# Loading and scoring the first pair of heads one head at a time, in a windowed attention and gated MLP kernel

## The chip, the cores and the metric

The kernel runs on one core of a Trainium2 chip. The metric is the device time of one execution in microseconds (us). The core has a matrix engine (TensorE; PE for its matmuls and PEld for its weight loads in the profile), a vector engine (VectorE, DVE), a scalar engine (ScalarE, ACT), GpSimd (POOL) and a queue engine (SyncE, SP) from which nearly all transfers between HBM and the on-chip memory are issued. The engines run their own instruction streams in order and wait for each other by semaphores.

## The reference

For 8 sequences (batch) of 576 tokens, 8 heads of 64 channels each, attention is computed with a causal window, and its result goes through an MLP with a gate:

```python
scores = scale * np.matmul(q, k.transpose(0, 1, 3, 2))        # [8, 8, 576, 576]
rel = pos[:, None] - pos[None, :]
mask_plain = (rel >= 0) & (rel < 32)                          # heads 0 to 3
mask_dil = (rel >= 0) & (rel < 128) & (rel % 4 == 0)          # heads 4 to 7
attn = softmax(np.where(masks, scores, -1e9))
x = np.matmul(attn, v) reshaped to [4608 tokens, 512]
h = x @ w_in                                                  # 512 -> 2048
return (h * sigmoid(1.702 * h)) @ w_out                       # 2048 -> 512
```

All inputs and the output are float32. Every query sees at most 32 keys.

## The kernel before, in words

Two heads are one "pair" (128 partitions: 64 channels of the one head, 64 of the other), so there are 32 pairs, four for each batch, numbered k = 0 to 31. `qk[k]` holds queries and keys of a pair, transposed, as 128 rows of 1152 floats. Pair 0 is the first thing that the kernel works on.

For a pair the steps are: load queries and keys (`load_qk`, line 425), load values (`load_v`, line 439), write the mask into a two-bank PSUM tile `sp` by a matmul with the identity (line 478) and add 42 small score matmuls for each head (line 490), both in `scores` (line 471); then on DVE the row maximum (line 510) and its subtraction out of PSUM (line 512, in the helper of line 353), on ACT the exponential (line 514), on DVE the sum and the reciprocal (lines 526 and 518), on POOL the two multiplications by it (line 529), on DVE two transposes (line 695), and the product with the values on PE (`first_product`, line 560, matmuls of line 576). The result is split into a high and a low part in `xs` by ACT (line 650) and DVE (line 652). The PSUM tile `sp` exists once: scores of pair k+1 start when the subtraction of pair k has read it. `first_product` writes a PSUM tile `first_x`, of which two pairs share the columns.

Weights come in as 64-bit words of w_in and w_out. `decode` (line 363) loads one 128 x 512 block (`fetch`, line 392) and turns it into a high and a low part: three operations that are ACT's for the first blocks (lines 402, 403, 396), shifts and adds on DVE or POOL (lines 406, 408), then the copy and the remainder (lines 409, 410). The MLP's up-projection (matmuls of line 863, three for each product, because high and low parts are multiplied apart) starts as soon as the first quarter of `xs` and the first w_in block are there. From then on PE is meant to be always busy.

What order the work has is written by a planner in the kernel's own code (`Plan`, lines 48 to 213). Every operation is given to it with a cost per engine that may do it, an urgency (the smaller, the earlier), the names that it reads and writes, a "slack" before which it isn't started, and, on PE, a count of instructions. `placed` (line 111) walks through time: it takes the engine whose next operation could start first, and among the operations that could start by then on this engine the one with the smallest urgency. Transfers go to SP's queue in the order of urgency as far as their inputs allow. For transfers it counts bytes over a common bus (line 203). The result is the program order of each engine; on the chip each engine keeps that order whatever the real durations are. The four first pairs have, for queries and keys, the urgencies -9.0, -5.7, -4.7 and -2.3, and for values -6.7, -6.7, -3.8 and -1.6 (the last three with a slack of 4, 11 and 14). The first weight blocks w_in 0, w_in 1, w_out 0 and w_in 2 have -7.8, -5.7, -4.6 and -2.5. `scores` of pairs 0 to 3 has an urgency of about -100000, so PE does it as soon as it can.

In the first 60 us the planner also fills PE's gaps with matmuls on constants (`warm`, line 1253): small ones of line 1262, each of which is two matmuls and two weight loads in the program, and large ones of line 1258. It keeps account of blocks of PE instructions: a first block of 193 and further ones of 256 (`fetched`, line 134), where the next block can be entered only some time after the last one was (4.2 or 6.1 in its own model); small fillers are put in up to such an edge (line 188).

The transfers' semaphores come from the framework, as do all waits: it follows which part of which tile an instruction reads and writes.

The functions that the change touches, and what calls them:

Of the kernel before, what the change touches and what calls it, by code (L numbers as in the profile page):

```python
# [15 lines left out]
B, H, S, D = 8, 8, 576, 64  # L16
DM, DF = 512, 2048
P = 128
NC = DM // P
NF = DF // P  # L20
GT = 512
# [12 lines left out]
QT = 5  # L34
# [182 lines left out]
def tile_windowed_attention_then_gated_mlp(  # L217
# [19 lines left out]
    add = plan.add  # L237
# [7 lines left out]
    def bank(shape, tag, name):  # L245
        return ps.tile(shape, F32, tag=tag, name=name)
# [116 lines left out]
    def decode(n, urgency):  # L363

        out_, f = order[n]
        if out_:
            src, hi, lo, key = w_out[f], wo(f)[:, 0], wo(f)[:, 1], f"wo{f}"
        else:
            src, hi, lo, key = w_in[f], wi(f)[:, 0], wi(f)[:, 1], f"wi{f}"

        r = n if n < 3 else (n - 2) % 5
        R, E = {3: "bt", 4: "qk0"}.get(n, f"cell{r}"), f"words{n % 3}"
        word = words[:, n % 3]  # L380
        taken = {5: ("first qk1",), 6: ("first qk1", "first v1")}.get(n, ())
        value = word.bitcast(F32)
        at = {}

        def fetch(e):
            if n == 3:
                raw = bt_all[:, 0:2 * DM].bitcast(U64)
            else:
                raw = temp([P, DM], U64, "qk", f"cell_{n}") if n == 4 else cells[r]
            at["halves"] = raw.bitcast(U16).rearrange("p (n t) -> p n t", t=4)  # L390
            at["low"], at["top"] = (raw.bitcast(U32).rearrange("p (n t) -> p n t", t=2)[:, :, j] for j in range(2))
            load(raw, src)

        def take_sign(e):
            if e == ACT:
                A.activation(at["halves"][:, :, 1].bitcast(F16), f32(at["top"]), AF.Copy, scale=2.0 ** -112)
            else:
                V.tensor_scalar(out=at["halves"][:, :, 1], in0=at["halves"][:, :, 3], scalar1=0x8000, scalar2=None,
                                op0=ALU.bitwise_and)

        add({DMA: 524}, {0: -7.8, 1: -5.7, 2: -4.6, 3: -2.5}.get(n, urgency), fetch, (), (R, R + "l", *taken))
        add({ACT: 0.66}, urgency, lambda e: A.activation(value, f32(at["top"]), AF.Copy, scale=2.0 ** -112), (R,), (E,))
        add({ACT: 0.66}, urgency, lambda e: A.activation(
            at["low"], at["low"], AF.Copy, scale=2.0 ** -29), (R,), (R + "l",))
        add({DVE: -0.75, ACT: 1.37}, urgency, take_sign, (R,), (R + "l",))
        add({DVE: -0.43}, urgency, lambda e: V.tensor_scalar(
            out=word, in0=word, scalar1=3, scalar2=None, op0=ALU.logical_shift_left), (), (E,))
        add({DVE: -0.70, POOL: 1.33}, urgency, lambda e: pair(e, word, word, at["low"], ALU.add), (R + "l",), (E,))
        add({ACT: 0.62, DVE: -0.42}, urgency, lambda e: copy(e, hi, value), (E,), (key,))
        add({DVE: -0.70, POOL: 1.36}, urgency, lambda e: pair(e, lo, value, f32(hi), ALU.subtract), (E,), (key,))  # L410
# [8 lines left out]
    def lots(k):  # L419

        if 0 < k < NC:
            return f"first qk{k}", f"first v{k}"
        return "qk0", "v0"

    def load_qk(k):
        u, place = pairs[k], lots(k)[0]

        def work(e):
            if 0 < k < NC:
                flat = (None, late, main_x, left_x)[k]  # L430
            else:
                flat = temp([P, 2 * S], F32, "qk", f"qk_{k}")

            u["qk"] = flat[:, 0:2 * S]
            load(u["qk"], qk[k])

        add({DMA: 590}, (-9.0, -5.7, -4.7, -2.3)[k] if k < NC else 1.6 * k - 2.0, work, waits(k), (place, place + "l"))

    def load_v(k):
        u, place = pairs[k], lots(k)[1]  # L440

        def work(e):
# [8 lines left out]
            u["v"] = flat.rearrange("p (a s d) -> p a s d", a=2, s=NB)  # L451
            load(flat, vp[k - NC])

        add({DMA: 390 if k < NC else 328}, (-6.7, -6.7, -3.8, -1.6)[k] if k < NC else 1.6 * k - 0.3, work, waits(k),
            (place, place + "l"), (0.0, 4.0, 11.0, 14.0)[k] if k < NC else 0.0)

    def waits(k):

        return ["xh3.0"] if NC <= k < FIRST * NC else []
# [8 lines left out]

        return k < FIRST * NC

    def scores(k):
        u = pairs[k]
        u["sp"] = bank([P, 2, GT], "sp", f"sp_{k}")
        u["all"] = u["sp"][:, :, 0:QT * W].rearrange("p a (t w) -> p a t w", t=QT)
        u["box"] = [u["all"][:, a] for a in range(2)]
        if masked(k):
            for a in range(2):
                T.matmul(u["box"][a], ident, plain if not dilated(k) else classes if k < NC else mask, start=True,
                         stop=False, skip_group_check=True)
        for t in range(QT):  # L480
            for a, g in [(a, g) for a in range(2) for g in range(4 if k < NC or t < QT - 1 else 2)]:
                rows = slice(D * a, D * a + D)
                dst = u["box"][a][32 * g:32 * g + 32, t]
                at = ROW * g + 32 * t if k < NC else HALF * (g // 2) + W * t + 32 * (g % 2)
# [198 lines left out]
    def first_attention(k):  # L683


        load_qk(k)
        load_v(k)
        add({PE: 1.5 if k else 2.3}, k - 1.0e5, lambda e: scores(k), (lots(k)[0],), ("sp", f"scores{k}"), count=180)
        softmax(k, k)

    def first_transposed(k):
# [621 lines left out]
```

## Time and profile before

| | us |
|---|---|
| median of 3 runs | 823.12 |
| lowest, highest | 821.65, 823.53 |
| the profiled execution's own time | 822.45 |
| its span in the profile | 820.7 |
| PE busy | 809.3 |
| DVE, ACT, POOL busy | 669.0, 518.0, 328.4 |
| PE's granted clock, mean | 0.997 |

The span runs from the first to the last instruction of the profile; the execution's own time is 1.75 us longer. "Busy" on PE includes the fillers, so the gaps of the start are not all seen in it. In rows of the timeline the first number is the start of a group in us, the second its length; a bracket says how long its engine idled before it and what ended that. In the chain of waits, "issue" is time in which an engine waited for nothing that the profile shows.

### The profile page before, as it was taken

The numbers are of one execution on the slowest core, as the hardware profiler recorded it, in microseconds if no ns is written. First come the engines' busy times: TensorE is split into PE (matmuls) and PEld (weight loads), VectorE is DVE, ScalarE is ACT, GpSimd is POOL, SyncE is SP. The second block draws the span as 40 slices with busy tenths as digits, with TensorE's granted clock in tenths as the row PEclk, the third lists the DMA queues.
The fourth block names the chain that finished last, engine by engine and source line by source line (L and its number), as shares of the span: only waits on it lengthen the run. The fifth ranks groups of instructions, "written<-read, shape, count | busy, mean of one in ns | idle before, by whom it ended". The sixth has DMA issues, their size and how long they took to land.

```text
span 820.7 us, 18890 instructions
## 1 busy us (share of the span) xinstructions
PE 809.3 (99%) x7279; PEld 653.4 (80%) x7279; DVE 669.0 (82%) x1081; ACT 518.0 (63%) x988; POOL 328.4 (40%) x294
## 2 busy tenths in 40 slices
PE   7999999999999999999999999999999999999997
PEld 4677878888887888778888888888888888888886
DVE  6898988888888876899889899996679885867575
ACT  7898986767577766786866654545456534544340
POOL 3442325455556553244345445531215332112251
PEclk9999999999999999999999999999999999999999
DMA  9577658899758657797788777775565658674545
GB/s 354 186 249 212 175 161 296 287 318 303 241 176 271 223 180 243 252 307 234 235 236 264 253 254 249 234 256 183 179 207 189 198 189 275 201 226 157 180 153 181
DMA packets 109610, 188.13 MB, mean 229 GB/s; under 512 B 26448, under 2 KB 55376, under 8 KB 109520
## 3 DMA queue, kind: packets, MB, share of 16 engines
q1 hardware_dynamic: 109376, 186.78, 70.2%
q8 instruction: 58, 0.95, 0.5%
q14 instruction: 32, 0.26, 0.1%
q10 hardware_dynamic: 144, 0.13, 0.0%
HBM read 140.64 MB, written 45.09 MB: 226 GB/s over the span
## 4 chain that ended last, share of the span: by engine, by line
PE 97%; DMA 1%; DVE 1%; issue 0%; ACT 0%; SPq 0%; DVEq 0%
PE hp_m L863 16%; PE up_p L1006 10%; PE up_r L1006 9%; PE up_q L1006 9%; PE acc_m L800 5%; PE second_p_Q L1121 5%; PE second_q_Q L1121 5%; PE acc_m L804 5%; PE acc_m L801 5%; PE second_r_Q L1121 5%; PE sp L490 4%; PE second_q_Z L1121 3%; PE second_r_Z L1121 3%; PE second_R L1121 3%; PE second_p_Z L1121 3%; PE av L608 2%
## 5 line engine op out<-in xcount | busy, mean ns | idle before, releaser
L353 POOL TENSOR_TENSOR arena<-arena 128x256 f32<-128x256 f32 (+3 forms) x94 | 100.7, 1083 | 97.8 <-DVE wi_last_units L353 21.6
L863 PE MATMUL hp_m<-xs,wi_kept 128*128 128x512 f32 x504 | 127.7, 396 | 1.2 <-DVE arena L872 0.9
L863 PEld LDWEIGHTS hp_m<-xs,wi_kept 128*128 128x128 f32 x504 | 92.9, 188 | 22.8 <-DVE arena L872 1.9
L353 POOL TENSOR_TENSOR wo_kept<-arena,wo_kept 128x512 fp32r<-128x512 f32 x41 | 56.9, 1395 | 131.5 <-ACT wo_kept L346 84.9
L346 ACT ACTIVATE wo_kept<-arena 128x512 fp32r<-128x512 f32 x111 | 69.2, 630 | 40.7 <-PE second_r_Q L1121 10.9
L1006 PE MATMUL up_r<-wi_kept,xs 128*128 128x512 f32 x336 | 85.3, 389 | 0.0
L1006 PE MATMUL up_p<-wi_kept,xs 128*128 128x512 f32 x336 | 84.2, 394 | 0.2 <-DVE arena L353 0.2
L1006 PE MATMUL up_q<-wi_kept,xs 128*128 128x512 f32 x336 | 83.4, 389 | 0.0
L1006 PEld LDWEIGHTS up_p<-wi_kept,xs 128*128 128x128 f32 x336 | 62.1, 188 | 14.7 <-DVE arena L353 0.9
L1006 PEld LDWEIGHTS up_q<-wi_kept,xs 128*128 128x128 f32 x336 | 63.0, 188 | 13.3 <-DVE arena L1028 0.3
L1006 PEld LDWEIGHTS up_r<-wi_kept,xs 128*128 128x128 f32 x336 | 63.1, 188 | 13.1
L353 DVE TENSOR_TENSOR wo_kept<-arena,wo_kept 128x512 fp32r<-128x512 f32 x80 | 61.1, 775 | 5.1 <-ACT wo_kept L346 4.7
L346 ACT ACTIVATE bt<-ct 32x256 f32<-32x256 f32 (+1 forms) x130 | 56.6, 435 | 11.7 <-DVE ct L534 6.0
L353 POOL TENSOR_TENSOR pr<-pr,sm 128x320 f32<-128x320 f32 x52 | 43.7, 856 | 48.5 <-DVE sm L518 43.5
L800 PE MATMUL acc_m<-gh,wo_kept 128*128 128x512 f32 x156 | 61.5, 394 | 0.0
L353 POOL TENSOR_TENSOR wo_kept<-wi_last_units,wo_kept 128x512 fp32r<-128x512 f32 x22 | 29.9, 1361 | 78.3 <-ACT wo_kept L346 72.3
L353 DVE TENSOR_TENSOR arena<-arena 128x512 f32<-128x512 f32 (+1 forms) x75 | 59.1, 797 | 2.7 <-ACT arena L346 1.8
L801 PE MATMUL acc_m<-gh,wo_kept 128*128 128x512 f32 x156 | 60.8, 390 | 0.0
L1027 ACT ACTIVATE arena<-arena 128x512 f32<-128x512 f32 x60 | 37.4, 628 | 33.4 <-DVE arena L353 27.2
L1028 DVE SCALAR_TENSOR_TENSOR arena<-arena 128x512 f32<-128x512 f32 x60 | 49.8, 837 | 1.7 <-ACT arena L1027 1.3
L346 ACT ACTIVATE gh<-arena 128x512 fp32r<-128x512 f32 x57 | 36.0, 631 | 17.5 <-DVE arena L872 5.8
L353 DVE TENSOR_TENSOR gl<-arena,gh 128x512 fp32r<-128x512 f32 x53 | 41.3, 779 | 6.5 <-ACT gh L346 3.2
(267 smaller groups left out, 1824.7 us busy)
## 6 DMA issues: line engine op xcount, KB each, us to landing
xs<-sums SPq DMA_DIRECT2D x168, 256.0 KB, 3.3
out_weights<-sums_o SPq DMA_DIRECT2D x63, 512.0 KB, 3.5
qk<-qk_dram SPq DMA_DIRECT2D x29, 576.0 KB, 4.4
xs<-sums_o SPq DMA_DIRECT2D x21, 512.0 KB, 3.8
v<-vp_dram SPq DMA_DIRECT2D x28, 320.0 KB, 4.1
sums_o<-arena SPq DMA_DIRECT2D x32, 256.0 KB, 3.2
sums<-arena SPq DMA_DIRECT2D x32, 256.0 KB, 2.9
arena<-wi_dram SPq DMA_DIRECT2D x15, 512.0 KB, 4.7
```

The costliest lines, as they stand in the source:

```text
L346: A.activation(dst, src, AF.Copy, scale=scale)
L353: (V if e == DVE else G).tensor_tensor(out=dst, in0=a, in1=b, op=op)
L490: T.matmul(dst[:, w:w + n], u["qk"][rows, at:at + 32], u["qk"][rows, S + first:S + first + n], start=not masked(k), stop=True, tile_positi ...
L608: T.matmul(u["x"][i][rows, at:at + last - first], u["v"][keys, a, m], bt[keys, m, a, first:last], start=(bank_, a) not in begun, stop=True ...
L800: T.matmul(self.acc[j], w[:, 0, cols], high, start=f == 0, stop=False)
L801: T.matmul(self.acc[j], w[:, 1, cols], high, start=False, stop=False)
L804: T.matmul(self.acc[j], w[:, 0, P * j:P * j + P], low, start=False, stop=f == NF - 1)
L863: T.matmul(hps[f], wi(f)[:, st, cols], mv[:, c], start=c == 0 and k == 0, stop=c == NC - 1 and k == 2)
L1006: T.matmul(self.banks[place], xs[:, slot, at:at + P], wi_kept[:, 2 * a + c, mv], start=fresh and c == 0 and k == 0, stop=c == 1 and k == 2 ...
L1027: add({ACT: 0.60}, -10.0, lambda e: A.activation(unit(tmp), src(), AF.Tanh, scale=0.851), need, own(tmp))
L1028: add({DVE: -0.70 if need[0][0] == "A" else 0.70}, -10.0, lambda e: V.scalar_tensor_tensor(out=unit(dst), in0=unit(tmp), scalar=1.0, in1=s ...
L1121: T.matmul(self.second[key], w[:, st, cols], mv, start=fresh and y == 0 and k == 0, stop=y == 1 and k == 2, skip_group_check=True)
```

## The change

Pair 0's `qk[0]` is loaded by two transfers of 64 rows (one head each) in place of one of 128 rows; they write two names, `qk0` and `head1`, have the same urgency (-9.0) and half the cost in the planner. `scores(0)` is given to the planner as two operations, one for each head, each with its own mask matmul and its 42 score matmuls, at a cost of 0.75 each where the whole had 2.3, and a count of 90 instructions each where the whole had 180. Head 1's operation waits for `head1`. Weight block 4, which is loaded into the same place as `qk[0]`, also takes `head1`. The urgency of pair 0's values goes from -6.7 to -4.5: in the order of urgencies they were third (behind qk 0 and w_in 0), and now qk 1, w_in 1, qk 2 and w_out 0 come ahead of them as well.

```diff
-        taken = {5: ("first qk1",), 6: ("first qk1", "first v1")}.get(n, ())
+        taken = {4: ("head1",), 5: ("first qk1",), 6: ("first qk1", "first v1")}.get(n, ())
...
-        def work(e):
+        def work(e, rows=slice(0, P)):
...
-            u["qk"] = flat[:, 0:2 * S]
-            load(u["qk"], qk[k])
+            if "qk" not in u:
+                u["qk"] = flat[:, 0:2 * S]
+            load(u["qk"][rows], qk[k][rows])
+        if k == 0:
+            for a in range(2):
+                add({DMA: 295}, -9.0, lambda e, a=a: work(e, slice(D * a, D * a + D)), (), (("qk0", "head1")[a],))
+            return
...
-        add({DMA: 390 if k < NC else 328}, (-6.7, -6.7, -3.8, -1.6)[k] if k < NC else 1.6 * k - 0.3, work, waits(k),
+        add({DMA: 390 if k < NC else 328}, (-4.5, -6.7, -3.8, -1.6)[k] if k < NC else 1.6 * k - 0.3, work, waits(k),
...
-    def scores(k):
+    def scores(k, heads=range(2)):
...
-            for a in range(2):
+            for a in heads:
                 T.matmul(u["box"][a], ident, plain if not dilated(k) else classes if k < NC else mask, start=True,
...
-            for a, g in [(a, g) for a in range(2) for g in range(4 if k < NC or t < QT - 1 else 2)]:
+            for a, g in [(a, g) for a in heads for g in range(4 if k < NC or t < QT - 1 else 2)]:
...
-        add({PE: 1.5 if k else 2.3}, k - 1.0e5, lambda e: scores(k), (lots(k)[0],), ("sp", f"scores{k}"), count=180)
+        if k == 0:
+            for a in range(2):
+                add({PE: 0.75}, k - 1.0e5, lambda e, a=a: scores(k, (a,)), (("qk0", "head1")[a],), ("sp", f"scores{k}"), count=90)
+        else:
+            add({PE: 1.5}, k - 1.0e5, lambda e: scores(k), (lots(k)[0],), ("sp", f"scores{k}"), count=180)
```

More of the change, by code (lines that the diff above doesn't have):

```diff
@@ L426, in load_qk @@
         u, place = pairs[k], lots(k)[0]
-        def work(e):
+        def work(e, rows=slice(0, P)):
             if 0 < k < NC:
                 flat = (None, late, main_x, left_x)[k]
-            else:
+            elif "qk" not in u:
                 flat = temp([P, 2 * S], F32, "qk", f"qk_{k}")
-            u["qk"] = flat[:, 0:2 * S]
-            load(u["qk"], qk[k])
+            if "qk" not in u:
[5 more added lines that the diff above has]
+            return
         add({DMA: 590}, (-9.0, -5.7, -4.7, -2.3)[k] if k < NC else 1.6 * k - 2.0, work, waits(k), (place, place + "l"))
@@ L469, in masked @@
         return k < FIRST * NC
-    def scores(k):
+    def scores(k, heads=range(2)):
         u = pairs[k]
-        u["sp"] = bank([P, 2, GT], "sp", f"sp_{k}")
+        if 0 in heads:
+            u["sp"] = bank([P, 2, GT], "sp", f"sp_{k}")
         u["all"] = u["sp"][:, :, 0:QT * W].rearrange("p a (t w) -> p a t w", t=QT)
```

## The prediction

> **What bounds the kernel now.** I read the page first, then the busy times by stretches.
>
> ```profile
> span 820.7 us, 18890 instructions
> 60.00:100.00 40.00, 40.00 (x391) 32.12 (x390) 35.65 (x64) 35.21 (x58) 12.94 (x11) 1.00 0.69 204
> ```
>
> From 60 us on PE (second number) is busy all the time. The change leaves that work alone, so it can move the end only by moving the start: by the time at which PE's real work, not its fillers, gets going. Next I read the chain of waits over the first 26 us.
>
> ```profile
> 1.25 4.70 DMA arena<-wi_dram
> 5.96 0.67 ACT arena L402
> 6.66 0.43 DVE arena L406
> 7.09 0.74 DVE mx L510
> 7.85 0.84 DVE pr L353
> 8.74 0.71 PE sp L478 x2
> 9.45 1.38 PE sp L490 x74
> 10.83 2.67 PE idle L1258 x6
> 13.50 0.53 PE sp L478 x2
> 15.10 2.27 PE idle L1258 x10
> 18.42 1.83 issue
> 20.62 1.42 PE first_x L576 x69
> 22.03 2.56 PE idle L1258 x6
> 24.60 1.09 PE first_x L576 x67
> ```
>
> Two things stand here. Pair 0's maximum (L510) starts at 7.09, not because its scores are late but because a weight operation (L406), fed by w_in 0, is ahead of it on DVE. And PE stops for 1.83 us in the middle of pair 3's scores, waiting for nothing that is seen. PE's timeline says what that is.
>
> ```profile
> 1.02 1.56 PE L1262 MATMUL idle<-ones 32*32 32x16 f32 x98 [1.02 <-DVE ones L309]
> 4.27 0.69 PE L478 MATMUL sp<-plain,ident 128*128 128x320 bf16 x2 [1.69 <-DVE plain L332]
> 4.89 1.45 PE L490 MATMUL sp<-qk 64*32 64x64 f32 x84
> 6.27 0.72 PE L1262 MATMUL idle<-ones 32*32 32x16 f32 x38
> 9.38 1.45 PE L490 MATMUL sp<-arena 64*32 64x64 f32 x84
> 13.97 1.13 PE L490 MATMUL sp<-arena 64*32 64x64 f32 x84
> 17.56 0.86 PE L490 MATMUL sp<-arena 64*32 64x64 f32 x65
> 20.25 0.37 PE L490 MATMUL sp<-arena 64*32 64x64 f32 x19 [1.83 <-issue]
> ```
>
> Up to the stop PE has run 98+2+84+38+2+2+84+6+2+84+10+2+65 = 479 matmuls (the 2s and the 2, 6 and 10 in between are masks and large fillers), and as many weight loads: 958 instructions. The plan's own account of instruction blocks has edges at 193, 449, 705 and 961. So the stop is a block that isn't there yet. Instruction 705 ran about 0.46 us into pair 2's scores, at 14.4; 961 ran at 20.25. A block behind the next edge thus took 5.8 us under full DMA. An estimate of the other end: after 20.25 come 19, 92 and 6 matmuls, 1192 instructions, and edge 1217 falls at about 24.7 without a stop, so there it took no more than 4.45, with a DMA share of 0.81 (the row of 20.80 below).
>
> **Head by head.** PE isn't held by the load of pair 0 for long. Its mask waits until 4.27 for DVE's `plain`, which the change doesn't touch; both masks and scores after that need 0.69 + 1.45, and they end at 6.34 now.
>
> ```profile
> 0.81 0.39 SPq L435 DMA_DIRECT2D qk<-qk_dram  x1
> DMA to landing us min/median/max: 4.1/4.1/4.1
> 45.74 0.43 PE acc_m L800
> 46.17 0.23 PE acc_m L801
> ```
>
> Queries and keys land at 0.81 + 4.1 = 4.9, when the masks are just done. Halved, they gain at most these 0.1 us. The new order mask, scores, mask, scores adds one change from small tiles back to a full one: the first full matmul behind scores takes 0.43, its like 0.23, so 0.20. Scores end at 4.27 + 0.69 + 1.45 + 0.20 = 6.6. For no gain, one more transfer is issued (0.39 of SP); it is hidden, as the loads queue on the DMA engines until 22 us.
>
> The real effect is on the order. In the planner's costs the scores of pair 0 now end about 1.45 earlier (0.75 behind head 1's half, where 2.3 stood), so the maximum and the subtraction go ahead of L406 on DVE. The subtraction ends at 6.6 + 0.05 + 0.82 + 0.02 + 0.84 = 8.35 in place of 8.69. L406 comes 1.7 later, and what hangs on it is w_in 0, first used at 25.6: free. Pair 1 follows: 8.40 + 0.71 + 1.38 = 10.5 in place of 10.83, if its keys are there by 9.1.
>
> **Values later.** The next rows give landings: first values, pair 1's keys.
>
> ```profile
> v<-first_v_dram SPq DMA_DIRECT2D x1, 384.0 KB, 6.2
> arena<-qk_dram SPq DMA_DIRECT2D x3, 576.0 KB, 7.1
> 1.71 0.44 SPq L448 DMA_DIRECT2D v<-first_v_dram  x1
> 2.19 0.43 SPq L435 DMA_DIRECT2D arena<-qk_dram  x1
> ```
>
> Values landed at 7.9, keys 1 at 9.3 (just ahead of the scores at 9.38), w_in 0 at 5.95. Without the values in front, keys 1 land 0.9 (384 of 576 KB by their 1.38) to 1.95 earlier, 7.35 to 8.4. By the urgencies the values are now behind keys 1, w_in 1, keys 2 and w_out 0, four transfers; the same bytes lie ahead of them as of w_out 0 now, so they land near 13.6. Their reader is `first_product` 0, now at 20.55: 7 us of cover; uncovered, it would cost what it lands behind that.
>
> **What takes the gain back.** Two steps, both from the order. On DVE pair 0's sum (L526) runs in the wait for pair 1's scores now:
>
> ```profile
> 7.22 1.34 ACT L396 ACTIVATE arena<-arena 128x512 f16<-128x512 f32 x1
> 9.48 0.83 DVE L526 TENSOR_REDUCE sm<-pr 128x10 f32<-128x650 f32 x1 [0.20 <-ACT pr L514]
> 10.87 0.82 DVE L510 TENSOR_REDUCE mx<-sp 128x10 f32<-128x640 f32 x1 [0.56 <-PE sp L490]
> 11.73 0.82 DVE L353 TENSOR_TENSOR pr<-sp,mx 128x640 f32<-128x640 f32 x1
> ```
>
> The exponential still waits for L396, ACT's weight step, until 8.56. In the planner's costs pair 1's maximum is now ready 0.05 ahead of that sum and so stands before it. With 0.82 and 0.83 of the rows, subtraction 1 then ends at 10.5 + 0.04 + 0.82 + 0.83 + 0.82 = 13.0, where 12.55 is now: 0.45 lost. PE didn't use 12.55, as fillers held it to 13.50; still, the lead is gone.
>
> Second, the blocks. With head 0 planned 0.82 earlier (295 of the bus's 360 a us), only 44 of the 49 double small fillers fit: 176 instructions, short of edge 193. It is now crossed by head 0's scores at about 4.7, not in the fillers at 2.5. Then 172 for the scores, 8 for four large fillers and 4 for masks: edge 449 lies 89 instructions of 168 into pair 1's scores, at 9.1 + 0.53 x 1.38 = 9.8. Plus 5.8: edge 705, inside pair 2's scores, at 15.6 (work alone would be there at 14.4). Plus 5.8: edge 961 at 21.4. With fewer fillers before it, it now lies 57 of 184 instructions into `first_product` 0 (now 38 ahead of it), so that product ends at 21.4 + 0.69 x 1.42 = 22.4, against 22.03: +0.4. Behind it the planner's gap takes 5 large fillers, not 6, of 0.43 each:
>
> ```profile
> 20.80:24.20 3.40, 3.40 (x95) 1.86 (x80) 3.28 (x7) 2.33 (x7) 1.21 (x1) 0.52 0.81 288
> 7.20:10.60 3.40, 2.75 (x87) 1.00 1.01 403
> ```
>
> These are stretches of 3.4 us: PE's busy time behind the length, then at the end the granted clock, the DMA share and GB/s (the second row has PE alone). The clock is halved in the 3.4 us behind the stop; it will be again. Minus 0.43: the sum is -0.03.
>
> Unknown is when the block behind edge 449 comes, as its predecessor is crossed at 4.7. With 4.45 it is there at 9.15 and costs nothing; with 5.8, at 10.5, everything behind is 0.7 later. The DMA of this stretch is as full as where 5.8 was measured, but the queue is filling up still at 4.7; I take about a third, +0.2. From `first_product` 1 on, the drains by ACT and DVE set the pace as now. The profiled execution took 822.45 (1.75 over its span); 822.65 after, and the median of before lies 0.67 higher: 823.3. Own range: -0.6 to +0.9, 822.5 to 824.0.
>
> **Rivals.**
>
> *Faster: no stop.* If blocks take 4.45 here too, pair 2's scores end at 14.5, subtraction 2 at 16.2, pair 3's scores at 17.9, and edge 961 (18.85) stops PE for only 0.5. `first_product` 0 ends near 19.9, 2.2 earlier; with PE always busy its clock stays full, and fillers of 0.23 no longer hold the next product. From 1.5 (values 2 land no earlier than now, near 23) to 2.9 gained: 821.0. For it: gaps between 4.27 and 9 close, and the values make room. Against: the 5.8, measured in just such traffic. The Trainium skill (Runtime: NRT & Kernel Launch, Instruction fetch mechanics) calls the crossing of a 256-instruction block mostly hidden; by that this rival would hold, yet the 1.83 above contradicts it.
>
> *Slower: a stop inside pair 1's scores.* In 7.20:10.60 PE idled 0.65 and the large fillers went on at 0.43 until 13.5. If the block behind 449 arrives at 10.5 or later, that idle time comes back and the clock stays halved; ten fillers, which the longer planned gap takes now in place of six, then last 4.3. Pair 2 starts at 15.5, its scores end at 17.6, edge 961 comes at 23.2, `first_product` 0 ends at 24.2: +2.2, less 0.43: 825.0. It decides from about 0.6 us of idling on.
>
> *Slower loads of half the rows.* No transfer of 64 rows is in this trace. If each half takes as long as the whole, head 1 lands 1.2 later (w_in 0, 512 KB, landed 1.05 behind the whole), at 6.1; scores end at 6.85, keys 1 land at 8.55 to 9.6, all edges move by up to 0.45: 823.8. For none of it is there a row; below nothing is excluded, the bytes being the same. The Trainium skill (SBUF — State Buffer, Door 1: The DMA port swizzle) has partitions 0 to 63 reach only half the ports, at half the rate, and two such transfers hardly overlapping; by it this rival is the case.
>
> *It doesn't do what it says.* If head 0's scores wait for both halves, they end at 4.9 + 0.72 + 0.20 + 0.35 + 0.72 = 6.9: +0.3, 823.6. Against: a half of a tile is followed by itself now, as DVE transposes after the first of two multiplications.
>
> ```profile
> 11.89 1.58 POOL L353 TENSOR_TENSOR pr<-pr,sm 128x320 f32<-128x320 f32 x2 [0.56 <-DVE sm L518]
> 12.82 0.50 DVE L695 STREAM_TRANSPOSE ct<-pr 128x320 f32<-128x320 f32 x1
> ```
>
> **Numbers.** Forecast 0.38, no stop 0.25, stop in pair 1's scores 0.20, slow halves 0.11, no effect of halving 0.06. 0.2% is 1.65 us, about what a measurement of this kernel can tell. Faster by more: most of the first rival and a tail, 0.23; slower by more: most of the second and tails, 0.20; within: 0.57. For 8 in 10 the range reaches to both: 820.9 (past the first rival's 821.0) to 825.2.
>
> **What would show it.** In the changed profile: L510 ahead of L406 on DVE, at 6.6; pair 1's scores ending at 10.5; L526 behind the second L510; 88 small fillers; "issue" gaps inside pair 2's scores near 15 and inside `first_product` 0 until 21.4. No gap at either would make it wrong on the fast side; a gap in pair 1's scores or fillers of 0.43 after 10.6, on the slow side; a head 1 landing after 5.5, on the loads.

## The result and the profile after

The changed kernel takes 830.24 us (829.22 to 832.88), the kernel before in the same comparison 823.04: a ratio of 1.0095 with a 95% interval of 1.0069 to 1.0122; by the medians that is 7.2 us slower. The prediction said 823.3 and no change. The profiled execution, the fastest of the four, took 829.22 us, with a span of 827.5, 6.8 over the span of before.

The page of the changed kernel: its span and the busy times.

```profile
span 827.5 us, 18826 instructions
...
PE 808.3 (98%) x7238; PEld 653.9 (79%) x7238; DVE 666.1 (80%) x1077; ACT 514.2 (62%) x985; POOL 337.5 (41%) x301
```

PE's busy time is not longer (808.3 against 809.3): the 6.8 us are idle time of PE. And POOL has 337.5 us of work where it had 328.4, though nothing in the change touches POOL. Where PE idles is read by stretches. The columns are the stretch, its length, PE's busy time and matmuls, the granted clock, the DMA share and GB/s. The changed kernel:

```profile
26.00:40.00 14.00, 11.47 (x286) 1.00 0.37 98
40.00:60.00 20.00, 19.02 (x218) 1.00 0.81 277
...
120.00:140.00 20.00, 18.39 (x215) 1.00 0.46 150
...
400.00:500.00 100.00, 98.61 (x828) 1.00 0.77 247
```

And the same view of the kernel before, for the stretches that changed most:

```profile
26.00:40.00 14.00, 13.78 (x208) 1.00 0.46 145
...
120.00:140.00 20.00, 20.00 (x231) 1.00 0.74 250
...
400.00:500.00 100.00, 100.00 (x829) 1.00 0.81 258
```

Somewhat more than half of the added idle time lies before 60 us, most of that behind 26; the rest lies far behind the change: PE, which was busy all of the time at 120 to 140 and 400 to 500 us, now idles there for 1.6 and 1.4. The waits of the changed kernel's PE (us in total, times, longest) say for what:

```profile
PE hp_m L874 <- DVE arena L883: 3.5, 3, 1.6
PE first_x L583 <- DVE xs L353: 2.5, 2, 1.3
...
PE first_x L583 <- issue: 1.7, 1, 1.7
PE second_p_Q L1132 <- DVE arena L1153: 1.4, 2, 1.2
PE sp L497 <- issue: 1.2, 1, 1.2
```

The kernel before has no wait of PE for DVE at `first_x` or at `second_p_Q` (the down-projection of the first full block), and at the up-projection `hp_m` only this one:

```profile
PE hp_m L863 <- DVE arena L872: 0.9, 1, 0.9
```

Only the two waits for "issue" belong to the steps that the prediction worked out. The others, 3.5 + 2.5 + 1.4, are waits for results of DVE.

The start as PE ran it in the changed kernel (timeline: start, length, instructions, idle time before in brackets):

```profile
4.70 1.32 PE L497 MATMUL sp<-qk 64*32 64x64 f32 x42
...
6.33 1.32 PE L497 MATMUL sp<-qk 64*32 64x64 f32 x42
...
10.09 1.33 PE L497 MATMUL sp<-arena 64*32 64x64 f32 x84
11.36 2.33 PE L1269 MATMUL idle<-ident 128*128 128x512 bf16 x10
...
14.49 0.99 PE L497 MATMUL sp<-arena 64*32 64x64 f32 x75
16.64 0.33 PE L497 MATMUL sp<-arena 64*32 64x64 f32 x9 [1.16 <-issue]
...
22.83 1.00 PE L583 MATMUL first_x<-ct,v 32*64 32x64 f32 x70 [1.72 <-issue]
...
29.90 1.08 PE L583 MATMUL first_x<-ct,arena 32*64 32x64 f32 x80 [1.22 <-DVE xs L353]
...
34.76 1.08 PE L583 MATMUL first_x<-ct,arena 32*64 32x64 f32 x80 [1.31 <-DVE xs L353]
...
42.47 1.25 PE L874 MATMUL hp_m<-xs,wi_kept 128*128 128x512 f32 x3 [0.94 <-DVE arena L883]
```

The two stops for "issue" stand where the prediction put them. PE has run 351 and 479 matmuls up to them, with the weight loads 702 and 958 instructions; 958 is also where the kernel before stops. The first product ends at 23.83 (22.04 before: +1.8). But then two stops of 1.22 and 1.31 follow that it did not have, both for `xs`, the result of draining `first_x` (ACT and DVE copy it out of PSUM), and one of 0.94 in the up-projection. The reason of the first stands on DVE, in the changed kernel's timeline:

```profile
26.32 1.23 DVE L406 TENSOR_SCALAR arena<-arena 128x512 uint32<-128x512 uint32 x2
...
28.59 0.59 DVE L353 TENSOR_TENSOR xs<-first_x,xs 128x432 fp32r<-128x432 f32 x1
```

Steps on weights (two L406 and, left out here, a remainder of 1.20) stand ahead of the drain that PE waits for. ACT's part of this drain is done at 27.69, DVE's starts at 28.59: 0.9 of the 1.22. The same, with some 0.7, is seen once more at 34.76. To follow the delay through the execution I use the first start of PE's matmuls for three tiles (tile view: count, ns of one, first and last start). Changed kernel, then before:

```profile
L811 PE MATMUL acc_m<-gh,wo_kept x156: 387/389/499, 43.6 to 333.7; 128*128 128x512 f32 x156
L1017 PE MATMUL up_p<-wi_kept,xs x336: 387/389/504, 342.7 to 482.7; 128*128 128x512 f32 x168
L1017 PE MATMUL up_q<-wi_kept,xs x336: 387/389/398, 487.1 to 634.4; 128*128 128x512 f32 x168
```

```profile
L800 PE MATMUL acc_m<-gh,wo_kept x156: 387/389/504, 39.6 to 330.6; 128*128 128x512 f32 x156
L1006 PE MATMUL up_p<-wi_kept,xs x336: 387/389/501, 337.9 to 477.2; 128*128 128x512 f32 x168
L1006 PE MATMUL up_q<-wi_kept,xs x336: 388/389/498, 480.2 to 627.5; 128*128 128x512 f32 x168
```

The delay is 43.6 - 39.6 = 4.0 when the down-projection of the first part starts, 4.8 at the first full block `up_p`, 6.9 at the next one, and 6.8 at the end of the span. So in these two executions 4.0 us are lost in the start and about 3 behind it, where the source of the kernel is unchanged.

What did change there is the order. By the lists that the planner writes, 206 of its 4184 operations are given to another engine than before, and 187 of these start behind 60 us of the planner's own time. The inputs that the change gave it (costs and counts of pair 0's loads and scores, one urgency) make it plan everything anew. How they reach so far stands in its code: it plans four times, and in the last three rounds, behind 130 us of its time, it goes no longer by the urgencies that are given to it but by latest starts that it works out from the start times of the round before (`latest`). By its own costs it expected the changed kernel to end 1.45 us earlier.

### The profile page after: what moved, and what is told of

Its sections match the earlier page's. It is cut to its first block, busy times and chain, and to the rows that moved or that the text cites. A ratio compares the mean times of both kernels' runs of the same rounds, so it can differ in the third digit from the quotient of the medians.

```text
span 827.5 us, 18826 instructions
## 1 busy us (share of the span) xinstructions
PE 808.3 (98%) x7238; PEld 653.9 (79%) x7238; DVE 666.1 (80%) x1077; ACT 514.2 (62%) x985; POOL 337.5 (41%) x301
## 4 chain that ended last, share of the span: by engine, by line
PE 89%; DVE 6%; ACT 2%; issue 2%; DVEq 0%; ACTq 0%
PE hp_m L874 14%; PE up_r L1017 9%; PE up_q L1017 9%; PE up_p L1017 8%; PE second_q_Q L1132 5%; PE second_r_Q L1132 5%; PE acc_m L811 5%; PE acc_m L815 5%; PE acc_m L812 5%; PE second_p_Q L1132 5%; PE sp L497 3%; PE second_r_Z L1132 3%; PE second_R L1132 3%; PE second_q_Z L1132 3%; PE second_p_Z L1132 2%; PE av L615 2%
## 5 line engine op out<-in xcount | busy, mean ns | idle before, releaser
L353 POOL TENSOR_TENSOR arena<-arena 128x256 f32<-128x256 f32 (+3 forms) x101 | 106.9, 1069 | 136.2 <-DVE wo_kept L353 28.4
L353 POOL TENSOR_TENSOR wo_kept<-arena,wo_kept 128x512 fp32r<-128x512 f32 x41 | 56.6, 1387 | 109.4 <-ACT wo_kept L346 80.9
L346 ACT ACTIVATE wo_kept<-arena 128x512 fp32r<-128x512 f32 x115 | 71.6, 629 | 39.8 <-PE second_r_Q L1132 10.5
L353 POOL TENSOR_TENSOR wo_kept<-wi_last_units,wo_kept 128x512 fp32r<-128x512 f32 x27 | 36.9, 1367 | 92.4 <-ACT wo_kept L346 84.9
L353 DVE TENSOR_TENSOR wo_kept<-arena,wo_kept 128x512 fp32r<-128x512 f32 x80 | 59.3, 755 | 5.4 <-ACT wo_kept L346 4.8
L353 POOL TENSOR_TENSOR pr<-pr,sm 128x320 f32<-128x320 f32 x52 | 44.4, 870 | 40.2 <-DVE sm L525 40.1
L353 DVE TENSOR_TENSOR arena<-arena 128x512 f32<-128x512 f32 (+1 forms) x72 | 53.9, 755 | 0.7 <-ACT arena L346 0.2
L346 ACT ACTIVATE wo_kept<-wi_last_units 128x512 fp32r<-128x512 f32 x46 | 29.0, 631 | 30.2 <-PE second_r_Z L1132 8.4
```

The lines of the kernel that those rows point to most:

```text
L346: A.activation(dst, src, AF.Copy, scale=scale)
L353: (V if e == DVE else G).tensor_tensor(out=dst, in0=a, in1=b, op=op)
```

## The experiments

**How they are built.** Ten of the kernels come from one source. It takes the changed kernel's operations, makes the planner's list from them (the "new" order), and makes a second list as the planner of before would (the "old" order: one load at 590, one `scores(0)` at 2.3, values at -6.7). Then it lays out one of them, or the one up to 60 us of the planner's time and the other behind. Two switches choose between the operations of the change and of before: `HALVES` (two loads of 64 rows) and `HEADS` (scores of a head apart). With both off and the old order everywhere, the instructions of every engine are in the order of the kernel before. Its core against the changed kernel, with the settings of the first experiment:

```diff
+EARLY, LATE, UNTIL = "new", "new", 60.0
+HALVES, HEADS = False, False
...
-                add({DMA: 295}, -9.0, lambda e, a=a: work(e, slice(D * a, D * a + D)), (), (("qk0", "head1")[a],))
+                add({DMA: 295}, -9.0, (lambda e, a=a: work(e, slice(D * a, D * a + D))) if HALVES else (
+                    lambda e, a=a: a == 0 and work(e)), (), (("qk0", "head1")[a],))
...
-                add({PE: 0.75}, k - 1.0e5, lambda e, a=a: scores(k, (a,)), (("qk0", "head1")[a],), ("sp", f"scores{k}"), count=90)
+                add({PE: 0.75}, k - 1.0e5, (lambda e, a=a: scores(k, (a,))) if HEADS else (
+                    lambda e, a=a: a == 1 and scores(k)), (("qk0", "head1")[a],), ("sp", f"scores{k}"), count=90)
...
-    for work, e in plan.ordered(warm, WARM, NC):
+    old = plan.as_before()
+    new_order = plan.ordered(warm, WARM, NC)
...
+    for _, work, e in chosen:
```

Lines in these kernels stand 24 to 37 further down than in the kernel before: L353 is L377 there, L406 L430, the scores are L522, the maximum L542, the first product L608, the up-projection L900, the large fillers L1295.

**1. The order alone.** New order, but one load of 128 rows and both heads' scores interleaved, as in the diff above.

> Every instruction stands in the order of the changed kernel, but pair 0's queries and keys come by one load of 128 rows and its scores are written with the two heads in turn, as before. Theory 'order' (the planner's new order costs, at the start and in the 120 to 500 us where PE idles 4.6 us in place of 1.2): near the changed kernel, 827 to 830. Theory 'operations' (the half loads at half the rate and the scores of one head alone at 29 ns a matmul in place of 17 cost, and the rest follows from them): back near the kernel before, 823 to 825.

Measured: 829.29 us, a ratio of 1.0072 (1.0054 to 1.0091): +6.1. None of the changed instructions is in this kernel, only the order that they led to. Its PE waits for DVE at the same places and as long as the changed kernel's (3.5 at the up-projection, 2.5 at the first products, 1.4 at `second_p_Q`), and its first acc_m comes at 42.7.

**2. The operations alone.** The other half: old order throughout, with half loads and heads apart.

```diff
-EARLY, LATE, UNTIL = "new", "new", 60.0
-HALVES, HEADS = False, False
+EARLY, LATE, UNTIL = "old", "old", 60.0
+HALVES, HEADS = True, True
```

> Every instruction stands in the order of the kernel before, but the load of pair 0 is issued as two halves and its scores are written head by head. Theory 'operations': scores of pair 0 end at 7.6 in place of 6.3 and w_in 0 lands up to 2.5 later, so first_product 0 ends 1.2 to 2.5 later and the time is 824.5 to 827. Theory 'order': within 1 us of before, 822.5 to 824.

Measured: 825.13, a ratio of 1.0024 (1.0013 to 1.0034): +2.0. The chain of waits in the start of this kernel shows the way:

```profile
0.80 0.62 SPq L460
...
1.48 0.58 SPq L460
...
2.11 5.96 DMA arena<-wi_dram
...
8.79 0.43 DVE arena L430
...
9.98 0.84 DVE pr L377
```

The two loads are issued in 0.62 and 0.58 where one took 0.39, and w_in 0 behind them lands at 8.1 and not at 5.95. In the old order its shift (L406, here L430) stands ahead of pair 0's maximum on DVE, so the subtraction ends at 10.82 and not at 8.69. This comes through to the end: the first acc_m stands at 41.3 (39.6 before), the first `up_p` at 339.5 (337.9), and the span is 1.6 longer in this execution.

**3 and 4. Half loads and lone heads, each by itself,** in the old order.

```diff
-HALVES, HEADS = True, True
+HALVES, HEADS = True, False
```

> The order of the kernel before; pair 0's queries and keys come as two loads of 64 rows, its scores are written with both heads in turn. In the run with both edits w_in 0 landed at 8.07 in place of 5.95, and the subtraction of pair 0, behind the weight shift that waits for it, ended at 10.8 in place of 8.7. Theory 'the half loads are the cost': all of the 2.0 is here, 824.8 to 825.5. Theory 'the lone heads are the cost': 823 to 823.7.

```diff
-HALVES, HEADS = True, True
+HALVES, HEADS = False, True
```

> The order of the kernel before, one load of 128 rows; scores of pair 0 are written mask, head 0, mask, head 1. With both edits the scores of one head took 1.2, where both heads in turn take 1.45, so they end at about 7.5 in place of 6.3, and the maximum, now at 7.1, starts at 7.6. Theory 'the half loads are the cost': 0.5 or less, 823 to 823.7. Theory 'the lone heads are the cost': 824.3 to 825.3.

Measured: the half loads 824.42, a ratio of 1.0016 (1.0007 to 1.0025): +1.4. The lone heads 822.75, 0.9998 (0.9988 to 1.0007): nothing. PE's timeline of the kernel with half loads, both heads interleaved:

```profile
4.89 0.44 PE L522 MATMUL sp<-qk 64*32 64x64 f32 x8
5.80 1.38 PE L522 MATMUL sp<-qk 64*32 64x64 f32 x76 [0.48 <-DMA qk<-qk_dram]
```

The second half lands at 5.8, where the whole landed at 4.9: halving the load made the last row of pair 0 come 0.9 later. Behind it w_in 0 lands at 8.2 and pair 0's subtraction ends at 10.95, much as with both edits, so the half loads explain that delay without the heads. PE's timeline of the kernel with lone heads:

```profile
6.45 1.31 PE L522 MATMUL sp<-qk 64*32 64x64 f32 x42
...
11.59 1.80 PE L1295 MATMUL idle<-ident 128*128 128x512 bf16 x6
...
20.24 0.37 PE L522 MATMUL sp<-arena 64*32 64x64 f32 x19 [1.37 <-issue]
```

Here the loads are those of before, and each head still takes some 1.25 us by itself, where both together took 1.38. Pair 0's scores end at 7.7 and not at 6.3, and pair 1's start 0.83 later. It costs nothing, for two reasons. The six fillers behind pair 1 took 1.80 us (2.67 before), so pair 2's scores start at 13.89 (13.97 before), and with them the edge inside them is reached, and the next block comes, at the same time as before: 20.24 (20.25). Pair 3's scores start 0.45 late again, and PE's stop in them is 1.37 and not 1.83: whoever reaches that edge later waits less.

**5 and 6. The new order in two parts.** First the changed kernel up to 60 us of the planner's time and the old order behind; then the kernel before up to 60 us and the new order behind.

```diff
-EARLY, LATE, UNTIL = "new", "new", 60.0
-HALVES, HEADS = False, False
+EARLY, LATE, UNTIL = "new", "old", 60.0
+HALVES, HEADS = True, True
```

> The changed kernel's operations and order for all that its planner starts before 60 us; from there on the order of the kernel before. The first down-projection starts 3.9 us later in the changed kernel (43.56 against 39.63). If the start carries its delay to the end and the rest of the order is at fault only for the other 3 us: 827.0. If the rest of the new order is as good as the old one and the delay of the start makes the later stops: 829 to 831. If the delay of the start is taken back later by slack: 823 to 825.

```diff
-EARLY, LATE, UNTIL = "new", "new", 60.0
+EARLY, LATE, UNTIL = "old", "new", 60.0
```

> The kernel before (one load, both heads in turn) with its own order for all that its planner starts before 60 us, and the changed kernel's order from there on. If the rest of the new order costs by itself: 826 (the 3.4 us of PE's added idle time after 60 us, less what the later start made of it). If the start alone is at fault: 823.

Measured: new start 828.49, a ratio of 1.0056 (1.0038 to 1.0074): +5.3. New rest 830.70, 1.0087 (1.0066 to 1.0108): +7.5. Each part costs by itself, the first between two of its forecasts, the second more than either of its own; and they don't add up: 5.3 and 7.5 against 7.2 for both. With the new rest, the first `up_p` starts at 342.7 in the second kernel, which has the start of before (its first acc_m at 40.9), and at 342.7 in the changed kernel, whose first acc_m is at 43.6. So in these two executions the 2.7 us that the better start gave to the new rest are lost on the way. Only part of that is seen: between the two points PE idles 3.8 us in the second kernel and 2.6 in the changed one, most of it waiting for DVE (3.0 and 2.5 at the up-projection). Where the rest goes, and which of DVE's operations between 60 and 340 us sets this pace, was not taken apart.

**7 to 10. Other ways of planning anew.** If the loss is the planner's new order, then other small changes of its inputs should show losses too. Each is one edit: only the values' urgency in the kernel before; only the cost of `scores(0)` in the kernel before; the changed kernel with a cost of the heads that lets the planner's end of pair 0's scores meet the measured one; and a number that has to do with neither, which the planner uses only in its later rounds.

```diff
-        add({DMA: 390 if k < NC else 328}, (-6.7, -6.7, -3.8, -1.6)[k] if k < NC else 1.6 * k - 0.3, work, waits(k),
+        add({DMA: 390 if k < NC else 328}, (-4.5, -6.7, -3.8, -1.6)[k] if k < NC else 1.6 * k - 0.3, work, waits(k),
```

> The kernel before with one number changed: pair 0's values have the urgency -4.5. The planner then writes 216 operations onto other engines, nearly all after 26 us. Theory 'order by itself' (any new order loses against the one that the kernel had, because costs and urgencies were settled on that one): slower by 2 to 7, 825 to 830, with stops of PE at DVE's results from 26 us on. Theory 'what the order is told' (only the score operations' costs, too short by 1.3 to 1.7, spoil it): 822 to 824.

```diff
-        add({PE: 1.5 if k else 2.3}, k - 1.0e5, lambda e: scores(k), (lots(k)[0],), ("sp", f"scores{k}"), count=180)
+        add({PE: 1.5}, k - 1.0e5, lambda e: scores(k), (lots(k)[0],), ("sp", f"scores{k}"), count=180)
```

> The kernel before with the planner's cost of pair 0's scores at 1.5 in place of 2.3, nothing else. Theory 'what the order is told': the maximum goes ahead of the weight shift (L406) and the sum of pair 0 behind the maximum of pair 1, drains of the first products find DVE taken, and 3 us are lost at the start: 826 to 829. Theory 'order by itself': also slower, 825 to 830, but with stops after 60 us as in the changed kernel. If the early order is harmless: 823.

```diff
-                add({PE: 0.75}, k - 1.0e5, lambda e, a=a: scores(k, (a,)), (("qk0", "head1")[a],), ("sp", f"scores{k}"), count=90)
+                add({PE: 2.2}, k - 1.0e5, lambda e, a=a: scores(k, (a,)), (("qk0", "head1")[a],), ("sp", f"scores{k}"), count=90)
```

> The changed kernel with a cost of 2.2 for each head's scores, so that the planner's end of pair 0's scores is 7.5, which the changed kernel's trace has (7.6). Theory 'what the order is told': the early order fits the chip again, only the operations' own 2.0 stay: 824.5 to 826. Theory 'order by itself': still 827 to 831.

```diff
-ROUNDS, SINCE, CALM, ROOM = 3, 130.0, 8.0, 3.0
+ROUNDS, SINCE, CALM, ROOM = 3, 130.0, 8.0, 3.1
```

> The kernel before with the planner's constant ROOM at 3.1 in place of 3.0: the same order to about 330 us, 141 operations on other engines behind that. The start is untouched. Theory 'order by itself': slower by 1 to 4 (PE stops in the first block after 340 us, as in the changed kernel): 824 to 827. Theory that late orders are all alike and only the start counts: 822.5 to 823.5.

Measured, against 823.12 for the kernel before (the last column is the profiled execution's first acc_m and first `up_p`, 39.6 and 337.9 before):

| edit | us | ratio (95%) | operations on other engines | acc_m, `up_p` |
|---|---|---|---|---|
| values at -4.5 | 829.15 | 1.0079 (1.0054 to 1.0105) | 216 | 41.6, 342.3 |
| cost of `scores(0)` 1.5 | 826.28 | 1.0042 (1.0026 to 1.0059) | 207 | 42.1, 340.9 |
| changed kernel, a head at 2.2 | 830.35 | 1.0090 (1.0075 to 1.0105) | 210 | 46.6, 347.4 |
| ROOM 3.1 | 826.51 | 1.0046 (1.0031 to 1.0061) | 141 | 41.3, 339.8 |

All four lose, by 3.2 to 7.2 us, and none of the first, second and fourth has a half load or a lone head in it. The planner doesn't see it: by its own costs they would end 3.7 later, 1.7 earlier, 0.8 later and 0.4 later. The second loses nearly all in the start (2.5 late at the first acc_m, 3.0 at the first `up_p` and 3.0 in its span), which is what the theory "what the order is told" said of it; but the third, which by that theory should have come to 824.5 to 826, is 7.0 late at its first acc_m. The last one has the same order as before up to about 320 us of the planner's time. Its profiled execution was its slowest (827.98): it is 1.7 late at the first acc_m without any new order (the last section shows how) and 1.9 at the first `up_p`, and loses 3.6 more behind. Among PE's waits in it is one that no other kernel here has at this place:

```profile
PE second_p_Q L1121 <- DMA out_weights<-sums_o: 1.2, 1, 1.2
```

So a cost nearer to the chip's doesn't help (the third), and the loss isn't special to this change. The waits differ from one order to the next; what is common is that they appear where the order of before had next to none. That any new order loses is not shown by five of them, only that these do.

**11 and 12. The values later, without planning anew.** The old order, the old operations, and one transfer moved by hand: pair 0's values go behind w_out 0 on SP's queue, which is where the change puts them. In the second kernel L406 of w_in 0 also goes behind pair 0's maximum and subtraction on DVE, as in the changed kernel.

```diff
+    for i, behind in ((2, 87),):
+        item = next(o for o in chosen if o[0] == i)
+        chosen.remove(item)
+        chosen.insert(next(j for j, o in enumerate(chosen) if o[0] == behind) + 1, item)
```

> The kernel before, in which one instruction stands elsewhere: on SP's queue the load of pair 0's values is behind those of keys 1, w_in 1, keys 2 and w_out 0. No cost or urgency is touched, so all else keeps its order. Keys 1 land 0.9 to 1.9 earlier, but pair 1's scores wait for the subtraction of pair 0 (8.69) and their masks: 822.7 to 823.3, no change. Theory 'order by itself' says that what the same move cost in a newly planned order (+6.0) is gone.

```diff
-    for i, behind in ((2, 87),):
+    for i, behind in ((2, 87), (30, 6)):
```

> As the run with the values moved, and on DVE the weight shift of w_in 0 (L406) stands behind the maximum and the subtraction of pair 0. These then end at 8.1 in place of 8.7, pair 1's scores at 10.2 to 10.4 in place of 10.8. If the blocks of PE's instructions follow (5.8 each), first_product 0 ends 0.4 to 0.6 earlier: 822.4 to 822.8. If the pace behind is set by other things, no change: 823. If any new order loses: 824 or more.

Measured: 822.67, a ratio of 0.9990 (0.9980 to 1.0000), and 822.62, 0.9993 (0.9985 to 1.0002). Moving the values costs nothing and may gain a few tenths; no more can be told. In the second kernel PE's stop in pair 3's scores moves up as meant, from 20.25 to 19.42, but what follows takes it back: its first acc_m is at 39.65, as before. PE's timeline:

```profile
19.42 0.37 PE L522 MATMUL sp<-arena 64*32 64x64 f32 x19 [1.92 <-issue]
...
24.42 1.09 PE L608 MATMUL first_x<-ct,arena 32*64 32x32 f32 x82 [0.48 <-issue]
25.44 1.66 PE L900 MATMUL hp_m<-xs,wi_kept 128*128 128x512 f32 x6
```

The next block's edge is now reached before the block is there, and the first hp_m starts at 25.44, where it was 25.62 in the kernel before. These two are the best of the versions tried, but neither beats the kernel before by more than its interval.

**13 and 14. What in the new start costs.** The new order up to 60 us and the old one behind, without half loads and lone heads; and the same with eight weight steps put behind the drains of `first_x`.

```diff
-EARLY, LATE, UNTIL = "new", "new", 60.0
+EARLY, LATE, UNTIL = "new", "old", 60.0
```

> The changed kernel's order up to the planner's 60 us, the order of before behind it, and the operations of before throughout (one load of 128 rows, both heads' scores interleaved). Theory A, the order of the start costs by itself: the run with the same order and the changed operations lost 5.3, of which the half loads can be 1.4 to 2.0; so +3.3 to +4.0, about 826.5 to 827.2, and the first acc_m matmul at 42.5 to 43.5. Rival B, the order of the start costs only where the half loads have made its inputs late: then within 0.2% of before, and the first acc_m by 40.9.

```diff
+    for these, behind in ((91, 99, 92, 93, 143), 74), ((129,), 79), ((101, 107), 80):
+        items = [o for i in these for o in chosen if o[0] == i]
+        chosen = [o for o in chosen if o[0] not in these]
+        at = next(j for j, o in enumerate(chosen) if o[0] == behind) + 1
+        chosen[at:at] = items
```

> As the run beside it (new start, old rest, operations of before), but in the start's order eight steps on weights (shifts, remainders and fractions on DVE and ACT) stand behind the drains of first_x that they stood ahead of. Theory A, these steps hold the drains up and so PE: the 1.2 and 1.3 stops of PE ahead of the first products 2 and 3 shrink to below 0.5 each, the first acc_m comes 1.5 to 2.5 earlier than in the run beside it, and so does the end. Rival B, the weights themselves are then late and take it back: the stops move to the hp_m matmuls of L900, and the first acc_m and the end stay within 0.7 of the run beside it.

Measured: 826.47, a ratio of 1.0042 (1.0029 to 1.0055), +3.1 on the 823.34 of its comparison; and with the drains first 828.86, 1.0067 (1.0047 to 1.0087), +5.5. So the order of the start costs by itself (theory A of the first), and the changed operations add the rest of the 5.3. But the cure made it worse. PE's timeline with the drains first:

```profile
28.65 1.08 PE L608 MATMUL first_x<-ct,arena 32*64 32x64 f32 x80 [0.35 <-DVE xs L377]
...
34.01 1.19 PE L608 MATMUL first_x<-ct,arena 32*64 32x64 f32 x80 [1.81 <-DVE xs L377]
35.12 7.16 PE L900 MATMUL hp_m<-xs,wi_kept 128*128 128x512 f32 x24
```

The first stop shrank from 1.22 to 0.35 as theory A has it, the second grew from 1.32 to 1.81. The 24 matmuls behind it took 7.16 and not 5.73, with PE's clock at 0.88 in this stretch, and the DMA moved 90 GB/s where it had moved 133. The two kernels' stretches from 26 to 40 us, first without and then with the drains first:

```profile
26.00:40.00 14.00, 11.46 (x200) 1.00 0.43 133
```

```profile
26.00:40.00 14.00, 11.84 (x257) 0.88 0.29 90
```

The first acc_m came at 44.4, 2.2 later than without. Neither theory had that. Some 1.0 of it is there before pair 1's product (25.55 against 24.59), where nine fillers took 3.12 and not 2.12, and 1.4 are the 24 matmuls. The second stop grew because the steps that were moved on DVE hold ACT: its copy for w_out waits 1.58 for them, and ACT's part of the drain, which stands behind that copy, starts at 31.55 and not at 30.37. So the weight steps ahead of the drains account for the first stop, but putting them behind moves the delay to the next one. Whether the lower clock is part of the order or of that one execution stays open.

## Why the prediction was wrong

**"The change leaves that work alone, so it can move the end only by moving the start."** This is the step that failed, and with the next one, which fails for the same reason, it makes most of the loss. The page showed PE busy from 60 us on, and the source behind is unchanged; but the order of that work is computed from all inputs, and some of them were changed. The prediction used the planner's costs to work out the new order of the first 25 us (L406 behind the subtraction, the sum behind the second maximum, 88 small fillers), and then took the old order for everything behind. The runs show +6.1 for the new order with the old instructions, and +7.5 for the new order behind 60 us alone; in the changed kernel's own trace some 2.8 of 6.8 us are lost behind the start. This could have been foreseen as a possibility: the other orders show that PE is always busy in the trace of before because of that order, and DVE is busy there 669 of 821 us, so it can be late.

**"From `first_product` 1 on, the drains by ACT and DVE set the pace as now."** Wrong for the same reason. The first product ended 1.8 late, and the first acc_m 4.0 late. From row to row the delay is 1.4 at pair 1's product (25.94 against 24.53), 2.5 at pair 2's, 3.1 at pair 3's and 3.9 at acc_m: the two stops of 1.22 and 1.31 for drains that stand behind weight steps in the new order, and the one of 0.94 in the up-projection. With the old operations the new start alone cost 3.1 in time.

**The blocks and the order of the start: right in kind.** L517 (the maximum) stands ahead of L406, the sum (L533) behind the second maximum, there are 88 small fillers, four large ones behind pair 0, ten behind pair 1; the stops for "issue" are inside pair 2's scores and inside `first_product` 0, as forecast, and not in pair 1's scores. From edge to edge a block took 16.64 - 10.8 = 5.8 and 22.83 - 16.64 = 6.2 us (the edge behind 89 of 168 instructions of pair 1's scores is worked out as in the prediction), where it had taken 5.8. Fillers behind pair 1 took 0.23 each, ten in 2.33, and behind `first_product` 0 there were nine, not five. The Trainium skill (Runtime: NRT & Kernel Launch, Instruction fetch mechanics) calls the crossing of such a block mostly hidden. At the edges 193 and 449 of the changed kernel PE shows no stop; at 705 and 961 the 1.16 and 1.72 us were not hidden.

**"Head by head" was mis-sized.** It took 0.72 for one head, half of the 1.45 for two, so that scores would end at 6.6; they ended at 7.58. A head alone takes 1.25 us, 42 matmuls of 1.25 / 42 = 30 ns, where the interleaved 84 took 1.38, 16 ns each (from the first start to the start of what follows; the rows' own lengths of 1.32 and 1.45 include the last one's tail). The kernel with nothing but lone heads shows the same 1.25, so it isn't the loads. This moved edge 449, and with it both stops, by the 1.0 us that the maximum was late, and with 0.4 for the second block the first product ended at 23.8 and not at 22.4. Taken alone it cost nothing in time, as faster fillers and a shorter stop took it up (experiment 4).

**"For no gain, one more transfer is issued (0.39 of SP); it is hidden": wrong.** The half loads took 0.62 and 0.58 to issue, and w_in 0 landed at 8.4 (5.95 before). The rival "Slower loads of half the rows" had the mechanism right, at 0.11: the rates in the changed kernel while the two halves ran, and before at the same time (GB/s in the last column):

```profile
4.00:4.50 0.50, 0.23 (x1) 1.00 1.07 220
4.50:5.00 0.50, 0.50 (x13) 1.00 1.05 159
```

```profile
4.00:4.50 0.50, 0.23 (x2) 1.00 1.02 405
4.50:5.00 0.50, 0.50 (x10) 1.00 1.05 377
```

The DMA engines are as busy, and move 159 to 220 GB/s where they moved 377 to 405. This agrees with the rule of the Trainium skill that the prediction quoted (SBUF — State Buffer, Door 1: The DMA port swizzle): partitions 0 to 63 reach half the ports, at about half the rate. The rival's price of +0.5 was too low: the half loads alone cost 1.4 in the old order, because what stands behind them in the queue comes later, w_in 0 first.

**"Values later" and the other rivals.** Seven us of cover for the values was right: nothing waited for them, and moved by hand they cost nothing. "No stop" was wrong, both stops came. The stop in pair 1's scores didn't come; that rival, moreover, took the 0.43 of the fillers until 13.5 for a halved clock, while the profile of before grants 1.00 from 10.8 to 13.5, so what slowed these fillers isn't shown. "It doesn't do what it says" was wrong too: eight matmuls of head 0 ran ahead of the wait for the second half in the kernel with half loads only, and in the changed kernel head 0's scores were done before head 1's began, without a stop of PE. No rival had the planner as its mechanism; that is why the range ended at 825.2.

## What to carry to other kernels

Where a planner writes the order, a change of one cost or urgency is a change of the whole program: before predicting, lay the two orders side by side to the end, and count an order that was good, with next to no waits, as something that a new one may lose (here five new plans lost 3.2 to 7.2 us). To try an idea, put it into the old order by hand first; here that separated later values worth nothing (-0.3 and -0.4 by the medians, not told from none) from a re-planning for the same move that cost 6.0. And half of a tile's rows is not half of its price: in this kernel its load and its matmuls each took nearly as long as the whole.

## What the runs showed of the hardware that was not expected

- Two transfers of 64 rows were slower to issue (0.62 and 0.58 us against 0.39) as well as to move (159 to 220 GB/s against 377 to 405). The transfer of 128 rows behind them was issued 0.85 later, took 0.58 to issue itself (0.42 before), and landed 2.1 to 2.5 us later. So the number of rows isn't shown to be what makes the issue slow.
- 42 small float32 matmuls of the one head (64 rows) took 1.25 us, 84 of both heads in turn 1.38.
- The same order of the start doesn't give the same start. In two kernels with before's order of the first 60 us (old start with new rest, and ROOM 3.1), the six fillers ahead of `first_product` 1 ran at full clock, PE reached the edge of the next block inside that product sooner, and stopped for it. The half clock came behind this stop, on the first six matmuls of the up-projection. The kernel with the old start and the new rest:

```profile
20.82 1.47 PE L1295 MATMUL idle<-ident 128*128 128x512 bf16 x6
...
24.67 1.20 PE L608 MATMUL first_x<-ct,arena 32*64 32x32 f32 x82 [1.36 <-issue]
25.79 2.93 PE L900 MATMUL hp_m<-xs,wi_kept 128*128 128x512 f32 x6
```

In the kernel before the fillers took 2.56 us, at half the clock, there was no such stop, and these six matmuls took 1.65 from 25.62 on. They start here only 0.17 later and end 1.45 later: the slow clock (0.68 granted from 24.2 to 27.6) fell on real work and not on fillers. The first acc_m is at 39.6 there, at 40.9 here and at 41.3 with ROOM 3.1, so 1.3 to 1.7 us of the start hang on which of the two happens, and an effect of this size in the start alone can't be read from one execution.
